# Holding two loads back behind a one-hot copy, and regrouping the argmax work of the first head pairs, in an attention and SwiGLU kernel

## The chip, the cores and the metric

The kernel runs on one core of a Trainium2 chip. The metric is the time of one execution on the device, in microseconds (us). The recorded span of the engines, which the profile pages show, is about 1.8 us shorter than that time.

## The reference

Attention over 4 batches of 8 heads, 768 tokens of 64 values each, masked by cluster: a query sees only keys whose nearest of 16 centroids is the same. Then an RMS norm and a SwiGLU block of width 1536 on the 3072 x 512 result.

```python
q_assign = np.argmax(np.einsum('bhsd,hcd->bhsc', q_n, c_n), axis=-1)      # k_assign likewise
mask = q_assign[:, :, :, None] == k_assign[:, :, None, :]
scores = np.where(mask, scale * np.matmul(q, k.transpose(0, 1, 3, 2)), -1000000000.0)
attn = ...softmax(scores)...
x = (attn @ v) as (3072, 512)
xn = x / rms(x) * rms_g
out = (silu(xn @ w_gate) * (xn @ w_val)) @ w_out
```

## The kernel before

The work goes by pairs of heads (16 pairs). One pair is prepared in thirteen parts. T0 to T3 are groups of three transposes on TensorE, each evacuated from PSUM by a copy to `qk32`. CAST turns the result to bf16 in `aug`, on GpSimd for all pairs but the first. SP is the product with the centroids (`sp`). TR, MX, CMP, SCL and BACK make one-hot rows of it on VectorE. PLACE copies these rows by DMA below the 64 rows of q and k in `aug`, so that the score matmul contracts over 80 rows and the mask comes out of it. CASTV casts v.

```python
def assign():                              # SP
    h0 = 2 * (pi % NP)
    sp = t_tile("sp")                      # one bank, shared with the transposes
    for j in range(4): nc.tensor.matmul(sp[32 * j:32 * j + 32, :], ...)
...
def place():                               # PLACE: four copies of 24 KB
    for a in range(2):
        for side in range(2):              # side 0: q, 1: k
            eng = nc.sync
            if pi == 0:
                eng = nc.gpsimd if side else nc.scalar
            elif pi == 1 and (a or side):
                eng = nc.gpsimd
            eng.dma_start(out=aug[st][a][D:KA, side, :]..., in_=ohT[r:r + 2 * NC, :])
```

The main loop goes in steps. A step issues one 512-wide score chunk (in the attention stretch three at a time into a three-bank tile `scw`, followed by one exp on ScalarE), one group of PV matmuls of the slot before, and, after six groups, the normalisation on VectorE that frees the only PV bank (`acc`). The extras, among them the parts above, are hung on steps by hand:

```python
for pi in range(4):
    load_pair(pi, (0, 1))                  # q and k of four pairs, SyncE queue
load_part(0, 2)                            # v of the first
...
nc.gpsimd.memset(zeros, 0.0)               # operand of the warm-up matmuls
...
w_ps = keep_warm(8)
p0[T0](); p0[T2](); keep_warm(2, w_ps); put_centroids(); p0[T1](); p0[T3](); ...
for i in (SP, TR, MX, CMP, SCL, BACK, PLACE):
    p0[i]()
...                                        # transposes of pairs 2 and 3, T0 of pair 4
at(2, p0[CASTV])
for i, step in ((SP, 0), (TR, 0), (MX, 1), (CMP, 2), (SCL, 2), (BACK, 3), (PLACE, 3), (CASTV, 5)):
    at(step, p1[i])
for i, step in ((T1, 10), (T2, 12), (T3, 15), (SP, 19), (TR, 20), (MX, 21), ...): at(step, p3[i])
for i, step in ((SP, 4), (TR, 5), (MX, 10), (CMP, 12), (SCL, 15), (BACK, 18), ...): at(step, p2[i])
...
for step in range(NT):
    slot, j = divmod(step, NCH)
    score_chunk(slot, j)
    ffn_next(...)
    if slot > 0 and 2 <= j < 2 + ST: pv_group(slot - 1, j - 2)
    if slot > 0 and j == 2 + ST:     pv_norm(slot - 1)
    extras(step)
```

In the code `p0` is the first pair, `p1` the second, and so on; the text counts from the first.

The softmax here doesn't subtract the row's maximum and nothing guards it: scores larger than these inputs give would overflow.

## Time and profile before

| what | value | from |
|---|---|---|
| time, first three runs | 343.6 us median (343.21 to 343.70) | results |
| time of the execution that was profiled | 344.86 us (span 343.1) | results |
| first score matmul | 15.17 us | chain of waits |
| eighth exp starts | 26.83 us | ScalarE's timeline |
| eleventh exp starts | 31.53 us | ScalarE's timeline |
| first FFN matmul | 64.24 us | TensorE's timeline |
| from there to the end of the span | 278.86 us | difference |

Three of these are marks: the first score matmul, the first FFN matmul and the end. The first says what the opening costs. The distance from it to the first FFN matmul says what the interleaving costs. The rest is FFN-bound, with TensorE nearly full. The profile page and the waits of before are shown in the prediction.

### The profile page before, as it was taken

What the parts mean: (1) busy time and instruction counts of PE and PEld (TensorE: products, weight loads), DVE (VectorE), ACT (ScalarE), POOL (GpSimd) and SP (SyncE); (2) the same over time, 40 slices, a digit from 0 to 9 for tenths busy, and PEclk for the clock granted to TensorE, in tenths of its full rate; (3) what the DMA queues carried; (4) which work ended last, traced back from release to release, by engine and by line L of the source; (5) the groups of instructions that cost most, each with busy time, mean ns of one, the idle gap of its engine ahead of it and who ended that gap; (6) DMA issues with size and microseconds to landing.
All of it is one profiled execution on the core that took longest, in us unless ns stands there. A gap on an engine that the chain in (4) does not pass through costs nothing.

```text
span 343.1 us, 7530 instructions
## 1 busy us (share of the span) xinstructions
PE 333.1 (97%) x2955; PEld 203.1 (59%) x2955; DVE 222.6 (65%) x460; ACT 225.5 (66%) x388; POOL 89.2 (26%) x123
## 2 busy tenths in 40 slices
PE   8799999999999999999999999999999999999996
PEld 4456666666666565666656566666666654555553
DVE  5687697698764777866465567774554687655540
ACT  4498999978777687766767677777777343323322
POOL 2667696066431133230111205010000011000000
PEclk9999999999999999999999999999999999999999
DMA  7757999909844125161501003120000022300012
GB/s 234 240 161 214 234 254 252 266 18 166 217 149 132 50 70 158 44 183 42 172 4 42 32 11 79 38 52 32 32 14 20 31 56 55 78 31 31 32 62 92
DMA packets 36771, 34.99 MB, mean 102 GB/s; under 512 B 13520, under 2 KB 33664, under 8 KB 36736
## 3 DMA queue, kind: packets, MB, share of 16 engines
q1 hardware_dynamic: 30240, 29.20, 28.1%
q0 software_dynamic: 5984, 4.84, 9.2%
q10 hardware_dynamic: 512, 0.48, 0.5%
q8 instruction: 23, 0.38, 0.5%
q14 instruction: 12, 0.10, 0.1%
HBM read 28.61 MB, written 6.29 MB: 102 GB/s over the span
## 4 chain that ended last, share of the span: by engine, by line
PE 86%; DVE 6%; ACT 3%; DMA 2%; issue 1%; POOLq 0%; POOL 0%; DVEq 0%; ACTq 0%
PE gp L401 17%; PE vp L401 17%; PE dp L434 17%; PE sc L299 12%; PE acc L313 9%; PE tp L195 5%; PE scw L299 3%; PE sp L231 3%; ACT pT L302 2%; PE w_ps L129 1%; DMA xnT<-xn 1%; DMA aug<-ohT 1%; DVE oh L254 1%; DVE tr L238 1%; DVE qk L199 1%
## 5 line engine op out<-in xcount | busy, mean ns | idle before, releaser
L302 ACT ACTIVATE pT<-sc 128x512 bf16<-128x512 f32 x192 | 113.8, 598 | 45.5 <-PE sc L299 44.9
L410 DVE SCALAR_TENSOR_TENSOR uu<-th,gp 128x384 f32<-128x384 f32 x96 | 53.0, 552 | 66.5 <-ACT th L406 66.4
L401 PE MATMUL gp<-xnT,wg 128*128 128x384 bf16 x384 | 78.1, 325 | 0.5 <-DMA xnT<-xn 0.4
L401 PE MATMUL vp<-xnT,wv 128*128 128x384 bf16 x384 | 78.1, 325 | 0.2 <-DVE gvT L416 0.2
L434 PE MATMUL dp<-wo,gvT 128*128 128x512 bf16 (+1 forms) x300 | 75.9, 370 | 0.0
L406 ACT ACTIVATE th<-gp 128x384 f32<-128x384 f32 x96 | 47.3, 492 | 43.3 <-PE gp L401 40.7
L313 PEld LDWEIGHTS <-pT 128*128 128x128 bf16 x1152 | 57.2, 97 | 29.3 <-DVE x L323 2.6
L299 PE MATMUL sc<-aug 80*128 80x512 bf16 (+1 forms) x256 | 73.0, 327 | 0.0
L218 POOL CAST aug<-qk 64x768 bf16<-64x768 f32 x60 | 52.2, 869 | 52.5 <-DVE qk L199 34.4
L313 PE MATMUL acc<-vbf,pT 128*128 128x65 bf16 x1152 | 63.2, 194 | 1.3 <-DVE x L323 0.5
L416 DVE TENSOR_TENSOR gvT<-uu,vp 128x384 bf16<-128x384 f32 x96 | 52.6, 548 | 5.9 <-PE vp L401 0.8
L401 PEld LDWEIGHTS <-wg 128*128 128x128 bf16 x384 | 37.2, 97 | 30.7 <-issue 1.3
L302 ACT ACTIVATE pT<-scw 128x1536 bf16<-128x1536 f32 x32 | 44.9, 1457 | 5.8 <-PE scw L299 5.4
L401 PEld LDWEIGHTS <-wv 128*128 128x128 bf16 x384 | 37.1, 97 | 18.8 <-issue 0.6
L299 PEld LDWEIGHTS <-aug 80*128 80x128 bf16 x384 | 33.0, 97 | 18.7 <-issue 7.4
L434 PEld LDWEIGHTS <-gvT 128*128 128x128 bf16 x300 | 29.1, 98 | 24.4
L199 DVE COPY qk<-tp 128x384 f32<-128x384 f32 x40 | 21.8, 552 | 15.6 <-PE tp L195 15.4
L299 PE MATMUL scw<-aug 80*128 80x512 bf16 (+1 forms) x128 | 26.1, 325 | 1.7 <-DMA aug<-ohT 1.5
L358 POOL TENSOR_SCALAR ir<-ss 128x3 f32<-128x3 f32 x7 | 1.7, 237 | 95.5 <-ACT jk L344 83.6
L367 DVE SCALAR_TENSOR_TENSOR xn<-x,ir,g_b 128x512 bf16<-128x512 bf16 x24 | 20.3, 862 | 6.5 <-POOL ir L359 5.4
L223 POOL CAST vbf<-v_in 128x768 bf16<-128x768 f32 x16 | 13.4, 836 | 34.2 <-issue 33.8
L323 DVE TENSOR_TENSOR x<-acc,inv 128x384 bf16<-128x384 f32 x32 | 17.8, 557 | 1.1
(65 smaller groups left out, 209.4 us busy)
## 6 DMA issues: line engine op xcount, KB each, us to landing
q_in<-in_q_dram SPq DMA_DIRECT2D x16, 384.0 KB, 5.3
k_in<-in_k_dram SPq DMA_DIRECT2D x16, 384.0 KB, 6.2
out_dram<-ob SPq DMA_DIRECT2D x23, 256.0 KB, 2.0
v_in<-in_v_dram SPq DMA_DIRECT2D x15, 384.0 KB, 6.0
wg<-in_moe_w_gate_dram POOLq DMA_DIRECT2D x4, 384.0 KB, 10.4
wv<-in_moe_w_val_dram POOLq DMA_DIRECT2D x4, 384.0 KB, 11.2
wo<-in_moe_w_out_dram POOLq DMA_DIRECT2D x4, 384.0 KB, 7.9
aug<-ohT SPq DMA_DIRECT2D x57, 24.0 KB, 1.9
```

What stands on the lines that cost most here:

```text
L199: nc.vector.tensor_copy(dst, tp)
L218: nc.gpsimd.tensor_copy(aug[st][a][0:D, :, par * HS:(par + 1) * HS], qk32[0][par * D:(par + 1) * D, 2 * a:2 * a + 2, :])
L299: nc.tensor.matmul(sc[:, o:o + n], lhsT=ag[:, 1, kc * P:(kc + 1) * P], rhs=ag[:, 0, qo:qo + n], start=True, stop=True)
L302: nc.scalar.activation(pts[slot][:, j * CH:(j + nch) * CH], sc[:, :nch * CH], ACT.Exp, scale=scale)
L313: nc.tensor.matmul(acc[:, TORD[g], :], lhsT=pts[slot][:, kc * S + g * P:kc * S + (g + 1) * P], rhs=vb[:, a, TORD[kc], :], start=(kc == 0), ...
L323: nc.vector.tensor_tensor(x_t[b][:, :, h * D:(h + 1) * D], acc[:, :, 0:D], inv.to_broadcast([P, ST, D]), op=ALU.mult)
L367: nc.vector.scalar_tensor_tensor(st["xn"][:, tl, :], x_t[b][:, t, :], st["ir", m][:, tl:tl + 1], g_b, op0=ALU.mult, op1=ALU.mult)
L401: nc.tensor.matmul(pt[:, :HS], lhsT=w[:, dc, fc * P:(fc + 1) * P], rhs=xnT[b, m][:, :, dc, :], start=(dc == 0), stop=(dc == DC - 1))
L406: nc.scalar.activation(th, pt[:, :HS], ACT.Tanh, scale=0.5)
L410: nc.vector.scalar_tensor_tensor(uu, th, 1.0, pt[:, :HS], op0=ALU.add, op1=ALU.mult)
L416: nc.vector.tensor_tensor(gvT[half][:, fc, :], uu, pt[:, :HS], op=ALU.mult)
L434: nc.tensor.matmul(dp, lhsT=gvT[hf][:, f, tl * P:(tl + 1) * P], rhs=wo[:, f, cols], start=(f == 0), stop=(f == FC - 1))
```

## The change

It has four parts. The **opening**: the memset that the warm-ups need goes from GpSimd to VectorE, and nine warm-up matmuls stand in place of eight. The **loads**: the fourth pair's k and the second pair's v are issued only behind one of the first pair's one-hot copies, which moves to the same queue, so that bulk traffic is out of the way when the one-hot rows are copied. The **regrouping**: the fourth pair's four transpose groups go between the argmax parts of the second pair, whose product takes the PV bank, and the third and fourth pair's argmax parts come later. The **tail**: the norms of the last batch come one tail step earlier.

```diff
+    zeros = const.tile([P, 512], BF16, name="zeros")
+    nc.vector.memset(zeros, 0.0)
...
-    for pi in range(4):
+    for pi in range(3):
         load_pair(pi, (0, 1))
     load_part(0, 2)
+    load_part(3, 0)
...
-            sp = t_tile("sp")
+            if pi == 1:
+                sp = ps_pv.tile([P, HS], F32, name="sp", tag="acc")
+            else:
+                sp = t_tile("sp")
...
-                    if pi == 0:
+                    if pi == 0 and (side or not a):
                         eng = nc.gpsimd if side else nc.scalar
...
-    w_ps = keep_warm(8)
+    w_ps = keep_warm(9)
...
-    late[3, 0] = keep_warm(3)
+    load_part(3, 1)
+    load_part(1, 2)
+    w_ps = keep_warm(3)
     for i in (T0, T2, T1, T3):
         p2[i]()
-    p3[T0]()
-    load_part(1, 2, nc.scalar)
     p1[CAST]()
-    keep_warm(4)
+    keep_warm(5, w_ps)
...
-    for i, step in ((SP, 0), (TR, 0), (MX, 1), (CMP, 2), (SCL, 2), (BACK, 3), (PLACE, 3), (CASTV, 5)):
+    for i, step in ((T0, 2), (T1, 5), (T2, 8), (T3, 11), (SP, 20), (TR, 21), (MX, 22), (CMP, 23), ...):
+        at(step, p3[i])
+    for i, step in ((SP, 0), (TR, 0), (MX, 3), (CMP, 3), (SCL, 5), (BACK, 6), (PLACE, 6), (CASTV, 7)):
         at(step, p1[i])
-    ... p3: T1 10, T2 12, T3 15, SP 19, TR 20, ...
-    ... p2: SP 4, TR 5, MX 10, CMP 12, SCL 15, BACK 18, ...
+    ... p2: SP 13, TR 14, MX 15, CMP 16, SCL 18, BACK 19, ...
     for pi in range(2, 4):
-        at(3, lambda pi=pi: load_part(pi, 2))
+        at(6, lambda pi=pi: load_part(pi, 2))
...
-            early = (8, 8, 9, 9, 10, 11, 12) if b == B - 1 else ...
+            early = (8, 8, 9, 9, 10, 10, 11) if b == B - 1 else ...
...
+        if pi == 4:
+            steps = (-10, -7, -5, -2, 0, 0, 2, ...)      # was (-11, -8, -5, -2, 0, 0, 2, ...)
```

More of the change, by code (lines that the diff above doesn't have):

```diff
@@ L93 @@
     nc.scalar.dma_start(out=c_in[:, 0:D], in_=centroids.rearrange("h c d -> (h c) d"))
-    for pi in range(4):
+    for pi in range(3):
         load_pair(pi, (0, 1))
     load_part(0, 2)
+    load_part(3, 0)
     g_b = const.tile([P, DM], F32, name="g_b")
-    zeros = const.tile([P, 512], BF16, name="zeros")
-    nc.gpsimd.memset(zeros, 0.0)
     ident_f = const.tile([P, P], F32, name="ident_f")
@@ L188, in t_group @@
                 tp = ((ps_t, ps_pv)[g - 2]).tile([P, HS], F32, name="tp", tag=("t", "acc")[g - 2])
-            elif (pi, g) in late:
-                tp = late[pi, g][:, 0:HS]
             else:
@@ L494 @@
     at(2, p0[CASTV])
-    for i, step in ((SP, 0), (TR, 0), (MX, 1), (CMP, 2), (SCL, 2), (BACK, 3), (PLACE, 3), (CASTV, 5)):
+    for i, step in ((T0, 2), (T1, 5), (T2, 8), (T3, 11), (SP, 20), (TR, 21), (MX, 22), (CMP, 23), (SCL, 24), (BACK, 25),
+                    (PLACE, 25), (CAST, 25), (CASTV, 28)):
+        at(step, p3[i])
+    for i, step in ((SP, 0), (TR, 0), (MX, 3), (CMP, 3), (SCL, 5), (BACK, 6), (PLACE, 6), (CASTV, 7)):
         at(step, p1[i])
-    for i, step in ((T1, 10), (T2, 12), (T3, 15), (SP, 19), (TR, 20), (MX, 21), (CMP, 22), (SCL, 23), (BACK, 24),
-                    (PLACE, 24), (CAST, 24), (CASTV, 28)):
-        at(step, p3[i])
-    for i, step in ((SP, 4), (TR, 5), (MX, 10), (CMP, 12), (SCL, 15), (BACK, 18), (PLACE, 18), (CAST, 6), (CASTV, 14)):
+    for i, step in ((SP, 13), (TR, 14), (MX, 15), (CMP, 16), (SCL, 18), (BACK, 19), (PLACE, 19), (CAST, 8), (CASTV, 14)):
         at(step, p2[i])
     for pi in range(2, 4):
-        at(3, lambda pi=pi: load_part(pi, 2))
+        at(6, lambda pi=pi: load_part(pi, 2))
     at(8, lambda: load_pair(4))
@@ L515 @@
         else:
-            early = (8, 8, 9, 9, 10, 11, 12) if b == B - 1 else (9, 9, 10, 11, 12, 13, 15)
+            early = (8, 8, 9, 9, 10, 10, 11) if b == B - 1 else (9, 9, 10, 11, 12, 13, 15)
             plan = [(sumsq, early[:3], (0, 1, 2)), (inv, early[3:4], (0,)), (norm, early[4:], (0, 1, 2)),
@@ L525 @@
         steps = (-11, -8, -5, -2, 0, 0, 2, 3, 4, 5, 6, 7, 10)
-        if pi == 6:
+        if pi == 4:
+            steps = (-10, -7, -5, -2, 0, 0, 2, 3, 4, 5, 6, 7, 10)
+        elif pi == 6:
             steps = (-11, -8, -5, -2, 0, 0, 2, 3, 4, 4, 5, 6, 7)
```

## The prediction

> **What bounds the kernel now.** I read the page first (busy shares), then TensorE's waits, then the chain of waits that ended last, then the timeline of the first 32 us engine by engine.
>
> ```profile
> span 343.1 us, 7530 instructions
> PE 333.1 (97%) x2955; PEld 203.1 (59%) x2955; DVE 222.6 (65%) x460; ACT 225.5 (66%) x388; POOL 89.2 (26%) x123
> ```
>
> TensorE is busy 333.1 of 343.1 us, so all that can be won without removing matmuls is 10.0 us. By stretches it idles 3.3 us after the last matmul (drain, untouched here), 0.8 us between 64 and 340 us, and the rest before 64 us. There the limit is shared: from 15.17 to 64.24 us TensorE is busy 46.2 of 49.1 us and ScalarE 44.7. After 64 us TensorE is full, so whatever is won before it should arrive at the end undiminished. The first waits:
>
> ```profile
> PE scw L299 <- DMA aug<-ohT: 1.5, 1, 1.5
> PE w_ps L129 <- POOL zeros L101: 1.3, 1, 1.3
> ...
> PE gp L401 <- DMA xnT<-xn: 0.4, 1, 0.4
> ```
>
> The first is the wait for the first pair's one-hot rows. In the chain of waits it looks like this (start, length):
>
> ```profile
> 10.55 0.59 DVE ohT L259
> 11.14 0.30 issue
> 11.44 3.68 DMA aug<-ohT
> 15.12 0.05 issue
> 15.17 0.82 PE scw L299 x4
> ```
>
> A transfer of 24 KB takes 3.68 us here. The second pair's first one-hot copy on the same GpSimd queue, issued at 19.83 us with no bulk load moving, landed in 1.9 us. At 11.4 us the SyncE queue's loads still fill the 16 DMA engines (100% of their time in 11.4 to 11.7, 69% in 12.3 to 12.6, stragglers until 13.8), because the fourth pair's k and the first v were issued at 6.81 and 7.22 and landed after 6.4 and 7.5 us.
>
> After that, ScalarE's exp sets the pace, and it has two gaps over half a microsecond:
>
> ```profile
> 16.03 9.98 ACT L302 ACTIVATE pT<-scw 128x1536 bf16<-128x1536 f32 x7 [2.27 <-PE scw L299]
> 26.83 4.13 ACT L302 ACTIVATE pT<-scw 128x1536 bf16<-128x1536 f32 x3 [0.82 <-PE scw L299]
> 31.53 4.45 ACT L302 ACTIVATE pT<-scw 128x1536 bf16<-128x1536 f32 x3 [0.57 <-PE scw L299]
> ```
>
> Seven exps run without a gap (9.98/7 = 1.43 us each), then it waits for scores. The scores were late because the PV product could not reuse its accumulator until VectorE had normalised the last one, behind one-hot work:
>
> ```profile
> 22.58 0.81 DVE L248 TENSOR_TENSOR oh<-tr,mx 128x384 bf16<-128x384 f32 x1
> 23.66 0.56 DVE L199 COPY qk<-tp 128x384 f32<-128x384 f32 x1 [0.28 <-PE tp L195]
> 24.14 0.90 DVE L254 TENSOR_SCALAR oh<-oh 64x384 bf16<-64x384 bf16 x1
> 24.96 0.18 DVE L322 RECIPROCAL inv<-acc 128x6 f32<-128x6 f32 x1
> 25.17 0.56 DVE L323 TENSOR_TENSOR x<-acc,inv 128x384 bf16<-128x384 f32 x1
> ```
>
> **What the Trainium skill says.** "DMA: Bandwidth & Descriptors", section "Queues, rings and completion order": the queues of SyncE and ScalarE have rings on the same 16 DMA engines, and each engine takes turns between rings, a packet at a time. So a small copy on another queue does not pass bulk traffic freely. The trace agrees: 3.68 against 1.9 us. "SBUF — State Buffer", section "SBUF: two separate sides": VectorE's two-port operations and GpSimd lock each other out of a shared port. The trace agrees: the compare above took 0.81 us and the scale 0.90 while GpSimd was casting, against 0.59 and 0.25 us for the same shapes at 18.05 and 18.67 us. "TensorE: Matmul & The Clock Gate", section "What's actually happening": the clock doubles after about 3.4 us of activity. The eight opening warm-up matmuls start 0.43 us apart, those at 10.21 us run three in 0.64, so it agrees.
>
> **The change, part by part.**
>
> *Opening.* The memset that warm-ups wait for moves to VectorE, where one of 128x256 f32 took 0.27 us (GpSimd: 0.53). TensorE starts some 0.2 us earlier, but a ninth warm-up (0.43 cold, 0.21 warm) uses that up: zero.
>
> *First scores.* With one bulk load (393 KB, 1.05 us at the 374 GB/s that these loads show) fewer ahead of the one-hots, the engines should be nearly empty by 11.8 us. ScalarE's copy, issued at 11.16, and GpSimd's, issued at 11.44, should land in about 2.0 to 2.4 us, near 13.5; the fifth closing warm-up ends near 13.5 too. I choose 13.6 for the first score matmul, against 15.17: **1.55 us won**. If the straggling engines still hold the copies it is 1.0; best case 1.8. The held-back k lands near 11.8+3.4 = 15.2 us and is wanted near 16.4, so it costs nothing.
>
> *Between the first scores.* Here I walk the queues by hand, from the first score matmul as zero, with spacings of the trace: three-bank score group 0.65 (readable 0.85 after its start), one-hot product `sp` 0.79, a group of three transposes 0.36 (evacuated from 0.56 after start, 0.56 long), one PV group 0.18, VectorE steps 0.5 to 0.6 each. Before: the second score group starts at 1.54 and its exp follows the first (0.86+1.43 = 2.29) directly. After, a transpose group stands before it, so it starts at 1.90 and its exp at 2.76: a gap of 0.45. The transposes share one PSUM bank, each waiting for VectorE's evacuation, and the evacuations now stand between the max, compare and scale of the second pair. I get transposes at 1.54, 2.80, 4.5 and 5.9, score groups 3 to 5 at 3.2, 4.9 and 6.3, with gaps of 0 to 0.2 on ScalarE. The third pair's `sp` (now in step 13, not 4) then pushes the sixth group to 8.3 and its exp to 9.1, where the exp before ended at 8.6: a gap of 0.5. The normalisation follows the third pair's compare and ends near 10.85 (before: 25.73-15.17 = 10.56), then the fourth pair's `sp` takes 0.79, and the eighth exp starts near 12.7, against 26.83-15.17 = 11.66. So relative to the first score this stretch **loses 1.1 us**.
>
> *Second gap.* The fifth pair's first transposes move behind the normalisation, which frees the 0.43 us of idling before the copy at 29.21 us, but the next transposes wait for that copy. My walk has the eleventh exp at 17.2 to 17.7, against 31.53-15.17 = 16.36: a total loss between 0.85 and 1.3. I take 1.1 in all, so the second gap is neutral.
>
> *Last batch.* Norms one tail step earlier. TensorE waits 0.38 us for the transposed activations at 284.77 us:
>
> ```profile
> 284.77 0.81 PE L401 MATMUL gp<-xnT,wg 128*128 128x384 bf16 x4 [0.38 <-DMA xnT<-xn]
> ```
>
> VectorE does one FFN product (0.55 us) between the first and second norm; moving it behind issues the DMA about 0.5 us sooner: **0.3 won**.
>
> Sum of the walk: -1.55 + 1.1 - 0.3 = -0.75, so 342.85 us. My walk adds up every wait in queue order at its full size and is likely pessimistic: it charges the accumulator wait and the bank wait one after the other, and if the argmax parts that leave the stretch before the normalisation free VectorE by even one 0.56 us step, the loss shrinks to about 0.5. I therefore put the point at **342.5 us**, a gain of 1.1.
>
> **The rivals.** (1) *All won*: the one-hots land early and both ScalarE gaps (0.82+0.57) close because the normalisation no longer stands behind a contended scale. Then -1.55-1.1-0.3, about 340.6. For it: the scale (0.90) and its copy do move behind the first normalisation. Against it: the accumulator's next user comes behind a later `sp`, and a transpose group more (0.36) is in a stretch where TensorE was already 93% busy (10.12 of 10.83 us from 15.17 to 26). (2) *Nothing won in front*: completion latency, not bulk traffic, holds the one-hots; then they land at 15, the interleaving only costs, and the time is 343.6+1.1-0.3, about 344.4. Against it: 1.9 us at 19.83. (3) *Front won, PSUM bank lost*: transposes one by one through the bank stall TensorE by the full 0.85 to 1.3 and more: 342.9 to 343.4. For it: single bank, in-order VectorE. (4) *Weights late*: compute reaches the FFN 2 us sooner than its weights. Against it: the first gate and value quarters are issued from 36 to 43 us and land within 17, before 60, with use from 64 us.
>
> **Range and chances.** The front is worth 1.0 to 1.8, the interleaving between a gain of 0.9 and a loss of 1.5, the tail 0 to 0.4. These give 340.8 to 344.0 for eight in ten. The 2% line is 6.9 us off on either side: more than all idle before 64 us for a gain, and no part costs as much, so faster and slower get one in a hundred each.
>
> **What would show it.** The first score matmul in the changed trace: 13.3 to 14.2 us (wrong if above 14.6). The GpSimd one-hot copy: 2.0 to 2.5 us. The second exp starting with a gap of 0.3 to 0.5 that was not there. The eighth exp 12 to 12.8 us behind the first score matmul; if it is at 11.0 to 11.5 the first rival is right. From there to 64 us the offset should stay. The 0.38 us wait near 284 us under 0.15. The prediction would be wrong if a load wait (k or v of the fourth pair) appears on TensorE, or if the offset at the first FFN matmul (64.24 us before) is not the offset at the end.

## The result, and the profile after

The changed kernel took 345.04 us in the median of four runs (344.76 to 345.46), the kernel before 343.65 us beside it (343.21 to 343.88). The ratio is 1.0043, with a 95% interval of 1.0026 to 1.0060: 0.4% slower, inside the 2% band, but above the upper end of my range (344.0) and on the other side of zero. Ratios here and below are the mean time of one kernel's runs over that of the other's of the same rounds, so not quite the ratio of the medians that I quote.

The page's first lines for the changed kernel do not show the loss at all:

```profile
span 343.0 us, 7504 instructions
PE 331.5 (97%) x2924; PEld 203.2 (59%) x2957; DVE 222.0 (65%) x461; ACT 225.3 (66%) x388; POOL 88.8 (26%) x122
```

The two profiled executions have the same span within 0.1 us, because the one of before was a slow draw (344.86 us) and the one of after an ordinary one (344.76 us). TensorE's busy time may not be compared either: 31 matmul records fewer are in this trace than in the other. So the reading goes by the three marks:

| | before | after | difference |
|---|---|---|---|
| start to first score matmul | 15.17 | 14.09 | -1.08 |
| first score to first FFN matmul | 49.07 | 49.82 | +0.75 |
| first FFN matmul to end | 278.86 | 279.09 | +0.23 |

The first part, in the chain of waits of the changed kernel (start, length, what):

```profile
10.70 0.58 DVE ohT L261
11.28 0.03 DVE qk L198
11.31 2.65 DMA aug<-ohT
13.96 0.14 issue
14.09 0.81 PE scw L301 x4
```

The copy that ends the wait takes 2.65 us where it took 3.68. It is another copy, too: before, GpSimd's landed last, here ScalarE's, issued at 11.31 us; GpSimd's, issued at 11.58, took 2.2 us. Next the middle, in ScalarE's timeline of the changed kernel (start, busy, operation, count, and in brackets the idle time before it):

```profile
14.94 1.45 ACT L304 ACTIVATE pT<-scw 128x1536 bf16<-128x1536 f32 x1 [1.65 <-PE scw L301]
16.85 5.58 ACT L304 ACTIVATE pT<-scw 128x1536 bf16<-128x1536 f32 x4 [0.46 <-PE scw L301]
23.07 2.79 ACT L304 ACTIVATE pT<-scw 128x1536 bf16<-128x1536 f32 x2 [0.64 <-PE scw L301]
26.62 4.13 ACT L304 ACTIVATE pT<-scw 128x1536 bf16<-128x1536 f32 x3 [0.75 <-PE scw L301]
31.50 4.45 ACT L304 ACTIVATE pT<-scw 128x1536 bf16<-128x1536 f32 x3 [0.74 <-PE scw L301]
```

Before, seven exps ran without a break. Now the run is broken three times before the eleventh exp starts: 0.46 behind the first exp, 0.64 behind the fifth, 0.75 behind the seventh. The eighth exp starts 26.62-14.09 = 12.53 us behind the first score, against 11.66 before. The eleventh starts 17.41 us behind it, against 16.36. TensorE's waits of the changed kernel (total, times, longest) say which tile was missing:

```profile
PE acc L315 <- DVE x L325: 1.5, 3, 0.7
...
PE tp L194 <- DVE qk L198: 0.8, 2, 0.5
PE vp L403 <- DVE gvT L418: 0.8, 2, 0.7
PE scw L301 <- DMA aug<-ohT: 0.4, 1, 0.4
```

The wait for the one-hot rows fell from 1.5 to 0.4 us. In its place TensorE waits 1.5 us for VectorE to free the PV bank (0.5 before) and 0.7 us, once, for a product bank in the FFN. That last one is in the tail. TensorE's and VectorE's timelines of the changed kernel around it:

```profile
277.98 0.81 PE L403 MATMUL gp<-xnT,wg 128*128 128x384 bf16 x4
279.48 0.81 PE L403 MATMUL vp<-xnT,wv 128*128 128x384 bf16 x4 [0.69 <-DVE gvT L418]
```

```profile
277.55 1.41 DVE L369 SCALAR_TENSOR_TENSOR xn<-x,ir,g_b 128x512 bf16<-128x512 bf16 x2 [1.34 <-POOL ir L361]
278.88 0.55 DVE L418 TENSOR_TENSOR gvT<-uu,vp 128x384 bf16<-128x384 f32 x1
```

And VectorE in the kernel before:

```profile
277.77 0.75 DVE L367 SCALAR_TENSOR_TENSOR xn<-x,ir,g_b 128x512 bf16<-128x512 bf16 x1 [1.35 <-POOL ir L359]
278.44 0.55 DVE L416 TENSOR_TENSOR gvT<-uu,vp 128x384 bf16<-128x384 f32 x1
278.90 1.41 DVE L367 SCALAR_TENSOR_TENSOR xn<-x,ir,g_b 128x512 bf16<-128x512 bf16 x2
```

Before, VectorE did one norm, then the product `gvT`, then two norms. Now both first norms stand ahead of `gvT`. That product is what frees the PSUM bank of the value matmuls, and TensorE comes for this bank before it is free.

### The profile page after: what moved, and what is told of

The parts are those of the page before. It is cut to its first block, busy times and chain, and to the rows that moved or that the text cites. A ratio compares the mean times of both kernels' runs of the same rounds, so it can differ in the third digit from the quotient of the medians.

```text
span 343.0 us, 7504 instructions
## 1 busy us (share of the span) xinstructions
PE 331.5 (97%) x2924; PEld 203.2 (59%) x2957; DVE 222.0 (65%) x461; ACT 225.3 (66%) x388; POOL 88.8 (26%) x122
## 4 chain that ended last, share of the span: by engine, by line
PE 83%; DVE 7%; ACT 3%; DMA 3%; issue 2%; POOL 1%; SPq 0%; POOLq 0%; DVEq 0%; ACTq 0%
PE gp L403 17%; PE vp L403 17%; PE dp L436 16%; PE sc L301 12%; PE acc L315 9%; PE tp L194 5%; PE sp L233 3%; PE scw L301 3%; ACT pT L304 2%; DMA aug<-ohT 2%; DVE oh L250 1%; DMA c_in<-in_centroids_dram 1%; DVE tr L240 1%; DVE ohT L261 1%; DVE mx L245 1%
## 5 line engine op out<-in xcount | busy, mean ns | idle before, releaser
L436 PE MATMUL dp<-wo,gvT 128*128 128x512 bf16 (+1 forms) x268 | 71.2, 369 | 1.7
```

The lines of the kernel that those rows point to most:

```text
L436: nc.tensor.matmul(dp, lhsT=gvT[hf][:, f, tl * P:(tl + 1) * P], rhs=wo[:, f, cols], start=(f == 0), stop=(f == FC - 1))
```

## The experiments

Twelve kernels ran. Kernels are compared only within the same rounds. Runs of the kernel before took 343.75 us in the median on the first chip (342.61 to 345.24, 11 runs), 343.84 on the second (343.25 to 346.48, 11 runs) and 344.44 on the third (344.13 to 346.03, 11 runs). Each kernel has six runs. All gave correct results. The kernel before was some 0.6 us slower in the third than in the other two, so that times expected there in us are best read through the ratio. I knew from the two traces that the 1.08 us of the opening could be a matter of which execution had been profiled.

### The kernel before again

No edit. This asks how much of the 15.17 us of the first score matmul belongs to the kernel and how much to the one execution.

> A control: the kernel before, unchanged. Its timed runs were 343.2 to 343.9 us, but the execution that I read before predicting took 344.86, 1.2 us more, while the changed kernel's profiled execution was one of its ordinary ones. Theory S (that execution was a slow draw in its opening: the one-hot wait is usually shorter): time 343.4 to 343.9, and this profile, if an ordinary execution, has a span near 341.9 and its first score matmul at 13.9 to 14.4 us, not 15.17. Rival T (the opening is always like that and the slow draw lies elsewhere): first score matmul again at 14.9 to 15.4.

Measured: 344.18 us (343.6 to 344.91), ratio 1.0010 (0.9986 to 1.0033). The first score matmul was at 15.04 us, so the rival's mark came and the theory's did not: a late first score is nothing special to the slow execution, since this one took an ordinary 344.15 us. It was late in another way, though: the one-hot rows came off VectorE 0.66 us later, and their copies took less (2.9 us for GpSimd's first, where it had been 3.7). TensorE's timeline tells the first half of it. The kernel before in the first trace:

```profile
4.69 0.89 PE L195 MATMUL tp<-ident_f,q_in 128*128 128x128 f32 x6
```

The same in this one:

```profile
4.69 1.49 PE L195 MATMUL tp<-ident_f,q_in 128*128 128x128 f32 x6
```

The same six transposes start at the same moment and take 0.6 us longer, because the clock had not yet doubled (by the clock records of the two traces, full clock is granted from 4.82 us there and from 6.18 us here). "TensorE: Matmul & The Clock Gate", section "What's actually happening", of the Trainium skill says that the window that decides this runs freely and doesn't start with the kernel, so it differs from run to run, and this pair of lines agrees. The 0.38 us wait for the transposed activations near 284 us was not there: the span from the first FFN matmul to the end is 278.59 us, not 278.86.

### The front alone

The kernel before with the opening and the loads of the change.

```diff
-    nc.gpsimd.memset(zeros, 0.0)
+    nc.vector.memset(zeros, 0.0)          # ahead of the centroids
-    w_ps = keep_warm(8)
+    w_ps = keep_warm(9)
+    ... k of the fourth pair and v of the second behind the one-hot copy, as in the change
```

> The kernel before with only the opening of the change: memset on VectorE with a ninth warm-up, one k and one v load behind the one-hot copy, that copy on SyncE. Prediction on record: 1.55 us won, so 342.1. Theory S: the first score matmul lies near 14.0 in both kernels, so the time is 343.4 to 343.8. Rival T: 342.3 to 342.8 (the changed kernel's first score matmul came 1.08 us sooner than in the profile of before).

Measured: 344.01 us (343.22 to 346.15), ratio 1.0010 (0.9976 to 1.0043). No gain shows, and the 342.3 to 342.8 us of the rival did not come. The first score matmul was at 14.81 us. The copies were quick (2.2 us for GpSimd's first), yet they were issued late, at 11.98 us. TensorE's timeline of this kernel:

```profile
1.18 4.02 PE L130 MATMUL w_ps<-zeros 128*128 128x512 bf16 x9 [1.18 <-DVE c_in L94]
4.99 1.41 PE L196 MATMUL tp<-ident_f,q_in 128*128 128x128 f32 x6
```

TensorE starts 0.12 us earlier than with the GpSimd memset (1.30), and the ninth cold warm-up then pushes the transposes from 4.69 to 4.99 us. In this execution a new wait appeared too:

```profile
PE tp L196 <- DMA q_in<-in_q_dram: 2.1, 1, 2.1
```

The fifth pair's q landed 7.3 us after its issue, where 4.8 to 5.5 us are usual. The stall costs more than its own length: behind it the trace shows TensorE at half its clock (granted 0.50 from 30.1 to 33.4 us, 1.00 before and after), and from first score to first FFN matmul it took 51.13 us, against 48.14 in the loads-alone trace below. These 3.4 us at half clock are what a mean granted clock of 0.995 stands for. Two of the six runs have it, the profiled one (346.15 us) and one of 346.13. The kernel before has such runs as well (345.23 us at 0.994, 346.48 and 346.03 at 0.995), so it occurs without the front part too, and six runs are too few to say whether it makes it more frequent.

### The regrouping alone

The kernel before with the regrouped parts of pairs two to five, and what goes with them (five closing warm-ups, the v loads of pairs three and four in step 6).

```diff
-    ... p1: SP 0, TR 0, MX 1, CMP 2, SCL 2, BACK 3;  p3: T0 in the opening, T1 10, T2 12, T3 15, SP 19
+    ... p1: SP 0 in the PV bank, TR 0, MX 3, CMP 3, SCL 5, BACK 6;  p3: T0 2, T1 5, T2 8, T3 11, SP 20
-    ... p2: SP 4, TR 5, MX 10, CMP 12
+    ... p2: SP 13, TR 14, MX 15, CMP 16
```

> The kernel before with only the regrouping between the first scores (transposes of the fourth pair in steps 2 to 11, second pair's products in the PV bank, later argmax of the third pair, warm-ups five, fifth pair's steps). My walk: 1.1 us lost, so 344.7, with the eighth exp 12.3 to 12.8 us after the first score matmul (before 11.66). Rival (interleaving is free or a gain): 343.6 or less, eighth exp at 11.7 or sooner.

Measured: 344.83 us (344.47 to 346.14), ratio 1.0037 (1.0011 to 1.0062): slower, with an interval that excludes 1. ScalarE's timeline of this kernel, where the first score matmul was at 14.61 us:

```profile
17.37 5.58 ACT L303 ACTIVATE pT<-scw 128x1536 bf16<-128x1536 f32 x4 [0.46 <-PE scw L300]
23.59 2.79 ACT L303 ACTIVATE pT<-scw 128x1536 bf16<-128x1536 f32 x2 [0.64 <-PE scw L300]
27.13 4.14 ACT L303 ACTIVATE pT<-scw 128x1536 bf16<-128x1536 f32 x3 [0.75 <-PE scw L300]
```

The eighth exp starts 12.52 us behind the first score, and the gaps are the same to the hundredth as in the whole change. The cost is thus a property of the order and not of the opening in front of it. From first score to first FFN matmul it is 49.81 us.

### The change without its tail

The changed kernel with the old steps of the last batch's norms.

```diff
-            early = (8, 8, 9, 9, 10, 10, 11) if b == B - 1 else ...
+            early = (8, 8, 9, 9, 10, 11, 12) if b == B - 1 else ...
```

> The changed kernel with the last batch's norms put back to their old steps. The prediction said that this part wins 0.3 us, so undoing it should cost: 345.3. What the changed kernel's trace shows is a wait of 0.69 us for a product buffer in place of one of 0.38 us for the transposed activations, so undoing it should win 0.3: 344.7. Rival: nothing, 345.0.

Measured: 344.47 us (344.07 to 344.93), ratio 1.0019 (0.9996 to 1.0041). In the trace the wait of 0.69 us for `gvT` is down to 0.2. The wait of 0.38 us for the transposed activations, which the tail was to remove, is not there either, although the norms are back at their old steps. From first FFN matmul to end the span is 278.38 us.

### The whole change again

No edit to the changed kernel.

> The changed kernel unchanged, as the reference for the next three on this chip, and for a second profile. Expected 344.8 to 345.2, with the gate/value wait for a product buffer (0.69 us near 279 us) in its trace again, and 12.5 us from first score matmul to eighth exp. If that wait is absent, it was a chance of one execution and the tail explains nothing.

Measured: 345.36 us (344.73 to 345.81), ratio 1.0031 (1.0002 to 1.0059). The loss comes again, and so does its make-up: the eighth exp at 12.53 us behind the first score, 49.83 us to the first FFN matmul, 279.03 us from there, with the 0.69 us wait in place. Only the opening differs: the first score matmul was at 15.04 us, 0.95 us later than in the first trace of the same kernel.

### The tail alone

The kernel before with the tail part of the change, the reverse edit of the one two above.

> The kernel before with only the last batch's norms one step earlier. Prediction on record: 0.3 us won, because TensorE waited 0.38 us for the transposed activations. In none of the four later profiles with the old norm steps was that wait there, so theory now: nothing to win, and the wait for the product buffer (0.69, with 0.2 of it there before) costs 0.5: 344.2 if the kernel before is at 343.7, and from first FFN matmul to end 279.0 us, not 278.3 to 278.6. Rival: 343.4, wait absent.

Measured: 344.67 us (344.23 to 345.42), ratio 1.0011 (0.9982 to 1.0040). The time alone can't tell, but the trace can. TensorE's timeline of this kernel:

```profile
279.48 0.81 PE L401 MATMUL vp<-xnT,wv 128*128 128x384 bf16 x4 [0.69 <-DVE gvT L416]
```

From first FFN matmul to end it took 278.98 us. (This execution also waited 1.4 us for the fifth pair's q, which landed 6.8 us after its issue. Its mean clock is 0.999: a stall of this length leaves no mark there.) All the kernels with the new tail lie between 278.98 and 279.09 us here, and all with the old one, apart from the first trace of before, between 278.28 and 278.59.

### The fourth pair's product one step earlier

The first of three tries to get the middle back. In the changed kernel the fourth pair's `sp` and its transpose go back to steps 19 and 20, so that `sp` comes before the normalisation again.

```diff
-    ... p3: (T3, 11), (SP, 20), (TR, 21)
+    ... p3: (T3, 11), (SP, 19), (TR, 20)
```

> The changed kernel with one thing moved: the fourth pair's one-hot product and its transpose one step earlier (19 and 20, as in the kernel before), so that TensorE does it ahead of the accumulator wait and not behind it. Theory (that order is what delays the eighth exp): from first score matmul to eighth exp 11.7 to 11.9 us in place of 12.5, to the eleventh 16.9 in place of 17.4, time 0.5 less than the changed kernel's. Rival (the shared bank with its added transposes is what costs): 12.4 or more, time unchanged.

Measured: 345.56 us (344.46 to 346.65), ratio 1.0037 (1.0003 to 1.0071). Half of it came as expected: the eighth exp starts 11.72 us behind the first score, 0.8 us sooner. But the eleventh starts 17.31 us behind it, hardly better than 17.41, and the time is no less than the changed kernel's (345.36 us), where 0.5 us less was expected. ScalarE's timeline of this kernel:

```profile
23.89 5.53 ACT L304 ACTIVATE pT<-scw 128x1536 bf16<-128x1536 f32 x4 [0.64 <-PE scw L301]
29.58 1.45 ACT L304 ACTIVATE pT<-scw 128x1536 bf16<-128x1536 f32 x1 [0.16 <-PE scw L301]
32.21 1.45 ACT L304 ACTIVATE pT<-scw 128x1536 bf16<-128x1536 f32 x1 [1.18 <-PE scw L301]
```

The 0.75 us gap in front of the eighth exp is gone, and the gap in front of the eleventh grew from 0.74 to 1.18 us. VectorE's timeline says why:

```profile
27.29 1.12 DVE L250 TENSOR_TENSOR oh<-tr,mx 128x384 bf16<-128x384 f32 x1
```

The fourth pair's compare takes 1.12 us where it took 0.59, since it now starts inside a cast of GpSimd, the first of a chain from 27.14 to 30.82 us. In the changed kernel it falls among these casts as well, but starts 0.05 us before one of them ends (13.01 and 13.06 us behind the first score). It stands ahead of the second normalisation, for which TensorE then waits 1.1 us.

### The same, with the fifth pair's transposes at their old steps

```diff
     ... p3: (SP, 19), (TR, 20) as above
-        if pi == 4:
-            steps = (-10, -7, -5, ...)
+        # pi == 4 again at (-11, -8, -5, ...)
```

> As the run before, and the fifth pair's transposes back to their old steps (one ahead). Theory (the second transpose group waits for a copy that now stands behind the normalisation): eleventh exp 16.4 to 16.6 us after the first score matmul, time 0.9 less than the changed kernel's. Rival (the move of those transposes was neutral, as I predicted): as the run before.

Measured: 345.18 us (344.79 to 345.6), ratio 1.0025 (0.9997 to 1.0053). The eleventh exp starts 17.13 us behind the first score, where I had expected at most 16.6, with a gap of 1.27 us. The fourth pair's compare took 1.12 us here too. The eighth exp is at 11.73 us. This fell as an explanation: the fifth pair's transposes are not what keeps the eleventh exp late. TensorE's wait moved with them: it now waits 1.1 us for VectorE's evacuation of one of these transpose groups, and hardly for the PV bank (0.3).

### The third pair's product early

The third pair's `sp` also in the PV bank, so that its argmax leaves the stretch before the normalisation.

```diff
-            if pi == 1:
+            if pi in (1, 2):
                 sp = ps_pv.tile([P, HS], F32, name="sp", tag="acc")
-    ... p2: (SP, 13), (TR, 14), (MX, 15), (CMP, 16)
+    ... p2: (SP, 7), (TR, 7), (MX, 9), (CMP, 11)
```

> The changed kernel with the third pair's one-hot product moved from step 13 to 7 (also in the PV bank), its transpose to 7, max to 9, compare to 11. In the changed kernel VectorE idles 0.77 + 1.27 + 0.49 us in this stretch, the largest while it waits for that product, and moving the fourth pair's product alone only moved the gap. Theory (VectorE's in-order work up to the second normalisation bounds the stretch, and the late product starves it): the 1.27 us idle is gone, eighth exp about 12.1 us and eleventh about 16.8 us after the first score matmul (12.5 and 17.4 in the changed kernel), time 0.6 less than the changed kernel. Rival (TensorE's added product pushes the early exps): eleventh exp still 17.2 or later.

Measured: 345.13 us (344.11 to 346.01), ratio 1.0014 (0.9995 to 1.0034). The eighth exp starts 11.93 us behind the first score, as expected. The eleventh starts 17.21 us behind it, which is what the rival said. VectorE's timeline of this kernel:

```profile
22.58 1.82 DVE L250 TENSOR_TENSOR oh<-tr,mx 128x384 bf16<-128x384 f32 x1
```

The third pair's compare takes 1.82 us, three times its undisturbed length, in the middle of GpSimd's casts (22.35 to 26.83 us). The idle time that the edit removed came back as blocked time. This execution was the slowest of its six (346.01 us). In it GpSimd's one-hot copy took 3.7 us and ScalarE's 4.2 in spite of the hold-back, and the first score was at 15.54 us: the last of the loads ahead of them landed only at 14.69 us.

### The fifth pair's loads first

An attempt on the stalls of the fifth pair's q, in the kernel before: its q and k are issued ahead of the v loads.

```diff
+    at(3, lambda: load_pair(4, (0, 1)))
     for pi in range(2, 4):
         at(3, lambda pi=pi: load_part(pi, 2))
-    at(8, lambda: load_pair(4))
+    at(8, lambda: load_part(4, 2))
```

> The kernel before, with the fifth pair's q and k loads issued ahead of the third and fourth pair's v. Three profiles showed a wait of 1.4 to 2.1 us for that q, which landed 6.8 to 7.3 us after its issue, and runs with a granted clock of 0.994 to 0.995 are those some 2 us slower. Theory (these slow draws are that wait): no run at a clock below 0.997 and none above 344.6; median 343.4 to 343.6. Rival: the slow draws stay, median as before.

Measured: 344.25 us (343.84 to 345.14), ratio 0.9992 (0.9974 to 1.0009). The "three profiles" of the expectation are two, the front alone (2.1 us) and the tail alone (1.4). No run fell below a granted clock of 0.999, so none shows that sign of the long stall, but six runs don't prove its absence. Two runs are above 344.6 us (344.69 and 345.14), against the theory, and the ratio shows no gain. The profiled execution had the latest opening but one (first score at 15.52 us, GpSimd's one-hot copy 4.3 us).

### The loads alone

The kernel before with the held-back loads, but with the old memset and the old eight warm-ups.

```diff
     ... k of the fourth pair and v of the second behind the one-hot copy, as in the change
     w_ps = keep_warm(8)                   # unchanged, as is the memset on GpSimd
```

> The kernel before with only the held-back k and v loads and the copy on SyncE, without the opening memset and the ninth warm-up. In the profiles so far GpSimd's first one-hot copy took 2.2 us in every changed opening, and 2.0, 2.0, 2.9 and 3.7 in the old one. Theory: copy 2.2 us, first score matmul 2.8 us after ScalarE's issue of its copy, first transposes at 4.69 as in the old opening (4.99 with nine cold warm-ups), so 0.3 us earlier than with the whole opening; time 343.4 to 343.7, not the 342.1 that I predicted for the front.

Measured: 343.99 us (342.47 to 345.03), ratio 0.9982 (0.9957 to 1.0008): no gain clear of noise, and 0.3 us above the expected range. The marks came as expected (copy 2.2 us, first transposes at 4.69, first score 2.83 us after ScalarE's issue). The profiled execution was one of the faster (342.91 us). The first score was at 14.55 us with a slow clock in the opening (the six transposes took 1.44 us), and TensorE did not wait for the one-hot rows. ScalarE's timeline brings a second effect:

```profile
25.59 4.13 ACT L303 ACTIVATE pT<-scw 128x1536 bf16<-128x1536 f32 x3 [0.21 <-PE scw L300]
```

The gap in front of the eighth exp is 0.21 us, not 0.82, so the eighth exp comes 11.04 us behind the first score. VectorE's timeline shows the cause, first of this kernel:

```profile
23.51 0.24 DVE L255 TENSOR_SCALAR oh<-oh 64x384 bf16<-64x384 bf16 x1
```

In the kernel before, the prediction shows the same instruction at 24.14 us with 0.90 us. It escapes GpSimd's casts, and the margin is tiny. Before, the third of them begins at 24.10 us, 0.04 us ahead of the scale; here it begins at 23.53 us, 0.02 us behind it. In the kernel before the casts begin 6.92 us behind the first score and the scale 8.97 us behind it (22.09 and 24.14 less 15.17); here it is 6.97 and 8.96 (21.52 and 23.51 less 14.55). The five old-order traces that I compared split cleanly: with 6.92 in three (the first trace of before, its repeat and the fifth pair's loads first) the scale takes 0.89 to 0.90, and with 6.96 and 6.97 (the front alone and this kernel) it takes 0.24. The tail-alone kernel, whose opening was early too (14.35 us), also has the 0.21 us gap, so held-back loads are not needed for it. In these traces it goes with an early first score (14.35 to 14.81 us, against 15.04 to 15.52); why the casts then come 0.05 us later is not shown.

### Loads alone, the fifth pair first, and one evacuation on ScalarE

The two edits above together, and the fourth pair's first transpose group evacuated by ScalarE, to take 0.56 us from VectorE.

```diff
-            on_dve = (... else g == 3 if pi == 2 else pi < 7 or g % 2)
+            on_dve = (... else g == 3 if pi == 2 else (pi, g) != (3, 0) and (pi < 7 or g % 2))
```

> An attempt to beat both: the kernel before with the loads held back, the fifth pair's q and k ahead of the v loads, and the fourth pair's first evacuation on ScalarE (with the loads held back, the first scores waited 0.3 us for VectorE's copy of it). Expected: first score matmul 2.5 to 2.7 us after the issue, no load wait, 342.9 to 343.3, no run above 344.3.

Measured: 343.50 us (342.28 to 344.5), ratio 0.9970 (0.9948 to 0.9992). This is faster than the kernel before by 0.3%, with an interval that just excludes 1; as one of twelve such comparisons it may be chance. The expectation was missed in its details: the first score came 2.78 us after ScalarE's issue (2.5 to 2.7 expected), the median is above 343.3 us, and two runs are above 344.3 (344.49 and 344.5). Nor do the runs tell which of the three edits did it. ScalarE's timeline of this kernel:

```profile
25.28 4.14 ACT L303 ACTIVATE pT<-scw 128x1536 bf16<-128x1536 f32 x3 [0.21 <-PE scw L300]
29.63 4.45 ACT L303 ACTIVATE pT<-scw 128x1536 bf16<-128x1536 f32 x3 [0.21 <-PE scw L300]
```

Both gaps are down to 0.21 us, and the eleventh exp comes 15.40 us behind the first score, against 16.36 before and 17.41 after. But this trace is of the fastest of its six runs (342.28 us, 1.2 us under their median), so some of this can be that run's own. This kernel did not run beside the changed one, so that it beats that one too rests on both having been measured against the kernel before (0.9970 against 1.0043 and 1.0031).

## Why the prediction was wrong

The three marks of all traces, set against the three terms of my sum:

| term | predicted | the two traces | several traces |
|---|---|---|---|
| opening and loads | -1.55 | -1.08 | -0.17 |
| regrouping | +1.1 | +0.75 | +0.94 |
| tail | -0.3 | +0.23 | +0.61 |
| sum | -0.75 | -0.10 | +1.38 |

The last column comes out like this. For the first row, the first score matmul of the five traces with the old opening (15.17, 15.04, 14.61, 14.35, 15.52) has a mean of 14.94 us, and of the seven with the new one (14.09, 14.81, 14.60, 15.04, 14.90, 14.39, 15.54) of 14.77. For the second row, from first score to first FFN matmul it is 49.82 us in the mean of four traces with exactly the change's order (49.82, 49.81, 49.82, 49.83), and 48.88 in three of the old one without a load stall and with a late opening (49.07, 48.77, 48.79). For the third, from there to the end it is 279.04 in the mean of the six with the new tail and 278.43 in that of the seven with the old one besides the first trace. The sum of +1.38 us stands against the timed differences of the means, +1.48 us (345.07 less 343.60) in the first comparison and +1.10 us (345.37 less 344.27) in the second. The match is rougher than it looks: the second row is taken against late openings alone. Against an early one it is +1.68 (49.82 less 48.14), and with two early openings in five, as in the first row, the sum would be about +1.7.

**The front term failed.** The step was "I choose 13.6 for the first score matmul, against 15.17: **1.55 us won**". The size was wrong on both ends. The 15.17 us, with its copy of 3.68 us, was one of the later of five draws; the same copy took 2.0 us in two traces with the old loads (the regrouping alone and the tail alone). And 13.6 was below every opening measured, of which the earliest was 14.09. The term that was too small there is the time from ScalarE's issue of its copy to the first score: 13.6-11.16 = 2.44 us in the prediction, 2.76 to 2.83 in eight of the nine held-back openings. GpSimd's copy did take the 2.2 us in all eight. But ScalarE's, the other that the first score needs, took 2.63 to 2.65, now that SyncE issues its copy (1.98 to 1.99) in the same moment; in the two quick openings with the old loads it had taken 2.0 and 2.1. It landed last.

The mean of -0.17 us comes apart in the same way. In the seven new openings ScalarE's copy was issued 0.29 us later than in the five old ones (11.76 against 11.47 us in the mean), and from there to the first score it took 0.46 us less (3.00 against 3.47). So the hold-back goes with shorter copies, as its mechanism said, but in few draws: the ninth held-back opening still took 4.34 us, and neither the front alone nor the loads alone was faster clear of noise. What I took for a property of the kernel was a coincidence of a clock that had doubled early, which makes the one-hot rows early, with loads that drained late.

**"Zero" for the opening failed too.** The ninth warm-up costs 0.3 us whenever the clock is still slow: the first transposes start at 4.99 instead of 4.69 us. I had put a cold warm-up at 0.43 us against 0.2 us gained, but called it zero. The start won only 0.12 us. The two traces of loads without the ninth warm-up have their first score at 14.55 and 14.23 us, the seven with it at 14.77 in the mean; two traces are too few to size that difference by itself, and the 0.3 us is the number that I trust.

**The regrouping was right.** The walk said an exp at 2.76 us behind the first score with a gap of 0.45: it was 16.85-14.09 = 2.76, with 0.46. It said a gap of 0.5 near the sixth exp: it was 0.64. It said the eighth exp near 12.7: it was 12.53. It said a total loss between 0.85 and 1.3: it was 0.87 at the eighth exp and 1.05 at the eleventh. One step was off: the normalisation, put at 10.85, ended at 10.54 us behind the first score, no later than before (10.56). The loss at the eighth exp is the fourth pair's product of 0.79 us, which now comes between; with that product ahead of the normalisation it was gone (11.72). One thing the walk could not tell: in the old order an early opening wins 0.62 us more behind the first score (eighth exp at 11.04 in place of 11.66 us), in the new order it does not (12.53 us with the first score at 14.09 and at 15.04 alike). So against an early opening the regrouping costs more, 49.82 less 48.14 us. Then came the step that spoiled it: "likely pessimistic ... I therefore put the point at 342.5". A walk that follows each queue in order does not err on the long side merely because it adds waits; almost all of the waits it added were there.

**The tail term failed in its sign.** The step was "moving it behind issues the DMA about 0.5 us sooner: **0.3 won**". The DMA was issued sooner, but the 0.38 us wait that this should cut was a chance of the one execution. It is absent in all seven other traces with the old tail. What I left out is what the moved instruction had been doing in its old place: the product `gvT` behind the two norms is the release of a PSUM bank, and TensorE waits 0.69 us for it in all six traces with the new tail, where it waited 0.2 us with the old.

**The base failed.** This is one mistake behind both failed terms. My sum began at the median of the timed runs, 343.6 us, while its terms were read from an execution that took 344.86 us. So it took the waits of a slow run off the time of an ordinary one: the 0.38 us wait belonged to that run alone, and of the 1.5 us wait a part. Set against the other traces, the first one is 0.23 us late at the first score (mean of the five old openings), 0.29 us longer from there to the first FFN matmul than the other two of late opening, and 0.43 us longer from there to the end: some 0.95 of the 1.26 us between it and the median.

Of the rivals, the second (nothing won in front, about 344.4 us) came closest to the time, but its reason, that completion latency keeps the copies until about 15 us whatever the loads, was not what was found: in the two quick openings with the old loads both copies had landed by 13.8 and 14.25 us. The first asked for an eighth exp at 11.0 to 11.5 us; it came at 12.53. Of the stalls that the third expected at the shared bank, TensorE had 0.4 us before the eighth exp. The fourth, late weights, did not happen. "From there to 64 us the offset should stay" held: the regrouping's loss of 1.05 us at the eleventh exp is what is missing at the first FFN matmul against the repeat of before (49.82 less 48.77). From there to the end the offset did not stay, because of the tail.

Four things stay open. Why the loads land so differently from one execution to the next (the second pair's q between 5.2 and 7.1 us after its issue) is not shown by anything here. The copy's landing fits the larger of "issue plus some 2 us" and "last load's landing plus 0.3 to 0.5 us" in the traces that I checked, which is a pattern seen and not one tested. Whether a regrouping exists that keeps its transposes and loses nothing is open too: the three tries moved the gap from the eighth exp to the eleventh, into compares blocked by GpSimd's casts. Which of the two held-back loads matters, and whether the copy's move to SyncE costs ScalarE's copy those 0.6 us, no run took apart. And whether the change makes stalls of the fifth pair's q rarer would take many more runs.

## What to carry to other kernels

Before reading a term from a profile, compare the time of the profiled execution with the timed runs: if it is slower than they are, some waits in it are that run's own, and a second profile of the same kernel tells which; if it is faster, some waits of an ordinary run are missing. Trust a walk through in-order queues as it comes out, and don't correct it by a feeling. When an instruction moves ahead of another, ask what the overtaken one releases, as well as what the moved one will start sooner.

## What the Trainium skill lacked or had wrong

- "TensorE: Matmul & The Clock Gate", section "What's actually happening", lets the moment of the doubling vary by 500 ns either way. Here it varies more: by the clock records, full clock came between 4.28 and 6.46 us in the seven traces that open with eight warm-ups, 1.1 us either way. The section also calls the warm-up penalty under 1% of a typical kernel's span. That agrees and lacks a word on small comparisons: the same six transposes took 0.82 to 1.49 us, and with the old opening the first one-hot copy behind them was issued between 10.90 us (where they took 0.82) and 11.96 us (where they took 1.49). That is 0.3% of the time and nearly as large as the effect of the whole change.
- "DMA: Bandwidth & Descriptors", section "Queues, rings and completion order", says that the engines take turns between queues but not how long a small copy takes when bulk loads precede it. Here a copy of 24 KB took 1.9 us with no load moving and 2.0 to 4.3 us with loads ahead of it, in executions of the same program too (3.7 and 2.9 us in two traces of the kernel before). Nor does it say what two small copies issued in the same moment take: here 1.98 to 1.99 us on SyncE's queue and 2.63 to 2.65 on ScalarE's, in eight traces.
- "SBUF — State Buffer", section "SBUF: two separate sides", has the lock between VectorE and GpSimd for the length of an instruction, for two-port operations and for those with two inputs in SBUF (the compare here is of the second kind). The runs agree, and add two numbers that it lacks: a compare of 0.59 us grew to 1.82 us within a chain of casts, by more than the 0.83 us of one cast, and 0.05 us in the phase of the two engines decided whether a scale took 0.24 or 0.90 us.
- No page that I read says how far two executions of one kernel on one core differ. Here 11 runs of the kernel before on one chip went from 343.25 to 346.48 us, at mean granted clocks of 0.995 to 1.0.
